# A gated linear recurrence and a squared-ReLU layer on one core: token rows laid out as 16 gaps, 96 head rows, 16 gaps, other transfers for weights and last heads, and a new order of the work up to group 4

## Chip, cores and metric

The kernel runs on one core of one Trainium2 chip. The metric is the device time of that core in microseconds (us): the median of repeated executions. Lower is better.

## What is computed

For 4 sequences, 8 heads, 768 steps and head size 48, a complex gated recurrence is run, and its output, 3072 tokens of 384 features, goes through two products with a squared ReLU between:

```python
S_re, S_im = a_re * S_re - a_im * S_im + k v^T,  a_re * S_im + a_im * S_re   # a limited to |a| < 0.999
y[t] = q[t] @ S_re
x = y as (3072, 384);  out = square(max(x @ w_in, 0)) @ w_out                 # w_in 384 x 2048, w_out 2048 x 384
```

The two weights arrive as 64-bit floats and are turned into 32-bit ones on the chip.

## The kernel before

Tokens are worked in 24 chunks of 128; two chunks are a group, so there are 12 groups (gi). A chunk's 8 heads lie as 4 pairs: in each half of the 128 partitions, rows 0 to 47 hold one head (`rows`), and the 16 rows after them are a gap (`pads`). Three pairs use the head rows. The fourth pair, the "last heads", is loaded into the gaps, a third of each head in each of three slots, so that the elementwise work has no empty rows. TensorE needs the last heads in head rows, so after the elementwise work `last_heads` (L879) copies them there by DMA, from the tile qk to the tile last. In the same way the features of the last heads in the token tile x are copied into its gap rows by `fill_gaps` (L1014), so that the first product has 3 full blocks of 128 rows.

All work is issued in an order written out by hand, the string list FRONT, which `follow` reads token by token; every engine takes its instructions in that order, and waits at the first one that isn't ready. The letters that matter, with group and step behind them:

- p, q: elementwise steps of chunk 0 and chunk 1 of groups 0 and 1 (o: of both chunks at once, from group 2). Steps 0 to 2 and 6 are ACT (squares L750, reordered copies L735); 3 is L764; 7 the inverse (L482, L782); 8 to 10 limit, lessened and grown factor on ACT (L735, L735, L796); 11 gates (L802, L482, L806); 13 grow (L822, L482); 15, 16 and 23 to 27 steps in blocks, 17 totals, 19 carried, 20 and 28 to 30 the four products that write qk (all L482 on DVE, the line of the helper tt); 21 the last heads' DMAs.
- a, b: chunk 0 and chunk 1 of a group on TensorE: 0 scores (L913, L921), 1 and 3 transposes (L928), 2 and 4 their copies on ACT, 5 the mask (DVE, L482), 6 sums of values (L947), 7 tokens into x (ACT, L956), 8 the state's products (L969) with the prod copy on POOL (L975), 9 the new state (DVE).
- g: gap copy. F and H: first product (L1022 by chunk, L1038 by group) and squared ReLU on ACT. T: second product of groups 0 and 1 (L1058). X, Y, Q, Z, R: second product of later groups (L1128), with sums on DVE.
- f, j: load of a block of weight words, block 0 to 7 of w_in and 8 to 15 of w_out; f on SP, j on POOL's queue, half of the rows of w_in each (L669). U, S (ACT, L600, L607), D, A (DVE, L614 and a custom instruction at L482): turning the words of a block into 32-bit floats. Three buffers hold words; a load waits for the buffer's earlier block.
- l, i: load of raw inputs (L507, gaps L517), v: of values (L528), s: store of results (L1092), M: memsets, mask and the first load of the activation table (L546 to L558).

SP's queue takes l, f, v, g, s and the last heads in the order of FRONT. TensorE's F of two chunks and four steps (F0.0.0 to F0.3.0) use blocks 0,1 / 2,3 / 4,5 / 6,7 of w_in.

A step of the elementwise work and the last heads' copies read:

```python
def last_heads():
    for hh in range(HH):
        for g in range(NG):
            at = slice(hh * ROWS + g, hh * ROWS + D, NG)
            nc.sync.dma_start(out=last[gi % 2][at, :, bs, 0:C + 1],
                              in_=qk[pads(hh), :, :, g, 0:C + 1])
```

Of the kernel before, what the change touches and what calls it, by code (L numbers as in the profile page):

```python
# [30 lines left out]
P = 128  # L31
# [395 lines left out]
def quotient_path(ctx, tc, feat, vtok, w_in, w_out, w1, w2, out, n_seq, count):  # L427
# [59 lines left out]
    vt = [const.tile([C, DM + PAD], F32, name=f"vt{i}") for i in range(2 * GC)]  # L487
# [55 lines left out]
    def turn_mask(step):  # L543
# [4 lines left out]
        if step > 1:  # L548

            for t in {2: [begun], 3: [t[:, :, :, :, C:W] for t in qk_of], 4: last,  # L550
                      5: [t[:, DM:] for t in vt] + prod, 6: kt, 7: states[0], 8: states[1]}[step]:
                nc.vector.memset(t, 0.0)
            return
# [14 lines left out]
    qk_of = [const.tile([P, 4, GC, NG, W], F32, name=f"qk{i}") for i in range(2)]  # L568
    last = [const.tile([P, 4, GC, W], F32, name=f"last{i}") for i in range(2)]
    prod = [const.tile([P, 3, GC, NP], F32, name=f"prod{i}") for i in range(2)]  # L570

    states = [[const.tile([P, 2, NP, ROWS], F32, name=f"state{b}{i}") for i in range(2)]
# [69 lines left out]

    def block(i):

        return order[i] == "2", order[:i].count(order[i])

    def fetch(i, second=False):
        of_w2, j = block(i)
        f, fbs = slice(j * BLK, (j + 1) * BLK), slice(j * 2, (j + 1) * 2)
        if (w_out if of_w2 else w_in).dtype == F32:  # L650
            if second:
                return
            if of_w2:
                nc.sync.dma_start(out=w2[:, fbs], in_=w2_view(w_out)[:, fbs])
            else:
                for at, gs, src in w1_views(w_in, D, crossed=True):
                    nc.sync.dma_start(out=w1_blocks[at, j, gs], in_=src[:, :, f])
            return
# [6 lines left out]
        else:  # L665
            for at, gs, src in w1_views(w_in, D, crossed=True):
                if (at.start >= ROWS) != second:
                    continue
                (other if second else nc.sync).dma_start(  # L669
                    out=words[at].rearrange("p (g f) w -> p g (f w)", g=NG)[:, gs],  # L670
# [41 lines left out]
    def make_operands(gi, only=None):  # L712
# [6 lines left out]
        qk, pd = qk_of[gi % 2][:, :, bs], prod[gi % 2][:, :, bs]  # L719
# [11 lines left out]
        by = [qk[:, i, :, :, 0:C].rearrange("p b g (j n) -> p (b g) j n", j=L) for i in range(4)]  # L731
# [116 lines left out]
        def carries():  # L848
# [5 lines left out]
            nc.scalar.copy(out=qk[:, 0:2, :, :, C], in_=at_end)  # L854
# [19 lines left out]
        def last_heads():  # L874
            for hh in range(HH):
                for g in range(NG):

                    at = slice(hh * ROWS + g, hh * ROWS + D, NG)
                    nc.sync.dma_start(out=last[gi % 2][at, :, bs, 0:C + 1],  # L879
                                      in_=qk[pads(hh), :, :, g, 0:C + 1])  # L880
# [11 lines left out]
    def chunk(gi, b):  # L892
# [7 lines left out]
        def scores():  # L900
            qk = qk_of[gi % 2]

            def operand(i, p_, at):
                return last[gi % 2][at, i, b, 0:C] if p_ == NG else qk[at, i, b, p_, 0:C]
# [3 lines left out]
            if not first:  # L908
                for two in range(0, NP, 2):
                    for c in (RE, IM):  # L910
                        for hh in range(HH):
                            for p_ in (two, two + 1):
                                nc.tensor.matmul(  # L913
                                    ys[p_ % 2][crossed(hh, p_), p_ // 2],
                                    lhsT=states[b][1 - c_seq % 2][rows(hh), c, p_],
# [9 lines left out]
        def keys_turned(c):  # L925
            tp = tiles["tp"] = pm.tile([C, NG, P], F32, tag="m", name="tp")
            for g in range(NG):
                nc.tensor.transpose(tp[:, g], qk_of[gi % 2][:, 2 + c, b, g, 0:C], ident)  # L928
# [14 lines left out]
        def sums_of_values():  # L943
            for p_ in range(NP):
                for hh in range(HH):
                    at = (HH * p_ + hh) * D
                    nc.tensor.matmul(tiles["y"][p_ % 2][crossed(hh, p_), p_ // 2],  # L947
                                     lhsT=v[:, at:at + ROWS], rhs=tiles["am"][:, hh, p_],
# [3 lines left out]
        def tokens():  # L952
            if gi not in x_of:
                x_of[gi] = ffn.tile([P, NP, TOK], F32, name="x")
            for odd in range(2):
                nc.scalar.copy(out=x_of[gi][:, odd::2, b * C:(b + 1) * C],  # L956
                               in_=tiles["y"][odd][:, 0:NP // 2])

        def added():
# [5 lines left out]
            for c in (RE, IM):  # L965
                for p_ in range(NP):
                    for hh in range(HH):
                        rr, at = slice(hh * ROWS, (hh + 1) * ROWS), (HH * p_ + hh) * D
# [3 lines left out]
        def last_products():  # L972
            bs = slice(b, b + 1) if gi < BY_CHUNK else slice(0, GC)
            pd, end = prod[gi % 2][:, :, bs], last[gi % 2][:, 0:2, bs, C]
# [4 lines left out]
        def new_state():  # L979
            before, new = [states[b][i][:, :, :, 0:D] for i in (1 - c_seq % 2, c_seq % 2)]  # L980
# [30 lines left out]
    def fill_gaps(i, b=None):  # L1011
        x = x_of[i] if b is None else x_of[i][:, :, b * C:(b + 1) * C]
        for hh in range(HH):
            nc.sync.dma_start(out=x[pads(hh), 0:NG], in_=x[rows(hh), NG])  # L1014
# [117 lines left out]
    def outputs(i, r):  # L1132
# [30 lines left out]
        "M7 M8 l0.0.0 M4 M2 M3 l0.0.1 M0 M1 p0.0 p0.2 p0.3 p0.4 p0.5 p0.7 q0.0 M6 q0.3 p0.9 "  # L1163
        "p0.8 p0.1 q0.4 p0.10 q0.5 p0.11 l0.1.0 f0 q0.7 i0.1.1 j0 i0.1.0 j1 j2 p0.12 p0.22 q0.8 "
        "q0.10 U0 q0.1 q0.9 q0.2 S0 f1 U1 S1 p0.15 p0.23 D0 p0.24 p0.13 p0.25 q0.11 p0.16 A0 "
        "p0.26 D1 f2 l0.1.1 f3 p0.27 M5 A1 p0.17 q0.22 p0.6 q0.13 p0.14 q0.12 q0.15 U2 p0.18 "
        "q0.14 S2 p0.19 q0.23 D2 l1.2.0 f4 i1.2.0 j4 j3 j5 q0.24 p0.28 q0.25 p0.20 q0.16 p0.29 "
        "q0.26 p0.30 q0.27 q0.17 a0.3 p0.21 a0.4 q0.6 i1.2.1 a0.1 p1.6 U3 q0.18 A2 U4 a0.2 S3 "
        "q0.19 D3 q0.28 q0.20 p1.0 S4 p1.3 p1.4 p1.5 a0.0 q0.29 q0.30 a0.5 v0.0 l1.2.1 f5 p1.1 "
        "p1.2 q0.21 a0.8 a0.6 p1.7 q1.0 a0.9 D4 A3 b0.3 b0.0 p1.8 a0.7 p1.10 p1.9 q1.1 U5 p1.11 "  # L1170
        "q1.3 A4 b0.5 p1.12 b0.4 S5 p1.15 p1.22 b0.1 b0.2 q1.4 p1.13 p1.23 D5 q1.5 j7 j6 g0.0 "
        "f6 f7 v0.1 q1.6 U6 p1.14 F0.1.0 S6 p1.24 A5 p1.25 D6 p1.16 U7 H0.1.0 S7 D7 p1.26 A6 "
        "p1.27 f9 f8 F0.2.0 b0.8 b0.6 A7 b0.7 H0.2.0 U9 U8 p1.17 p1.18 q1.7 F0.0.0 F0.3.0 "
        "H0.0.0 p1.19 D8 p1.20 p1.28 D9 p1.29 g0.1 f10 D10 p1.30 F0.3.1 q1.10 S8 H0.3.0 H0.3.1 "
        "S9 v1 f12 f11 q1.9 q1.2 A8 b0.9 F0.1.1 F0.2.1 A9 a1.1 T0.0.0 q1.8 U10 q1.11 a1.2 S10 "
        "U11 q1.12 D11 D12 q1.15 A10 q1.23 p1.21 a1.3 T0.1.0 a1.0 S11 q1.22 H0.1.1 f13 f15 "
        "F0.0.1 q1.13 q1.24 a1.5 q1.25 D13 q1.16 A11 a1.6 U12 a1.4 q1.14 S12 a1.7 a1.8 q1.26 "
        "A12 q1.27 q1.17 T0.2.0 T0.3.0 T0.4.0 U13 H0.2.1 H0.0.1 S13 q1.18 A13 g1.0 F1.3.0 i2 "
        "q1.19 q1.20 q1.28 q1.29 q1.30 f14 U15 U14 S14 H1.3.0 l2 q1.21 o2.0 S15 D14 D15 A14 "
        "o2.3 A15 o2.1 o2.4 o2.5 a1.9 o2.7 T0.5.0 F1.1.0 F1.2.0 T0.6.0 T0.7.0 b1.1 o2.2 E0.0 "  # L1180
        "b1.2 o2.8 o2.9 b1.0 b1.5 b1.3 H1.1.0 T0.0.1 T0.1.1 F1.0.0 o2.10 o2.11 o2.12 o2.15 b1.4 "
        "o2.23 o2.22 o2.13 o2.24 o2.25 o2.16 o2.26 b1.6 b1.8 T0.2.1 T0.3.1 T0.4.1 b1.7 o2.27 "
        "o2.17 T0.5.1 T0.6.1 T0.7.1 o2.14 H1.0.0 o2.6 E0.1 w0 g1.1 o2.18 o2.19 o2.28 o2.20 "
        "o2.29 o2.30 s0.0 l3 o2.21 v2 F1.1.1 H1.1.1 H1.2.0 T1.0.0 T1.1.0 F1.2.1 T1.2.0 T1.3.0 "
        "T1.4.0 T1.5.0 b1.9 a2.3 F1.0.1 o3.6 H1.2.1 a2.4 a2.1 T1.6.0 o3.0 o3.1 o3.3 a2.0 a2.5 "
        "a2.2 o3.4 o3.5 H1.0.1 o3.7 t0 T1.7.0 a2.6 a2.8 a2.7 b2.0 b2.5 a2.9 W0 o3.9 o3.8 o3.2 "
        "E1.0 F1.3.1 b2.3 b2.4 b2.6 T1.0.1 T1.1.1 T1.2.1 T1.3.1 H1.3.1 b2.7 g2 F2.1 F2.6 T1.4.1 "
        "T1.5.1 o3.10 o3.11 o3.12 o3.15 o3.23 o3.24 o3.25 o3.22 o3.13 o3.16 o3.26 o3.27 o3.14 "
# [182 lines left out]
```

## Time and profile before

| | |
|---|---|
| median of 3 runs | 670.68 us (669.2 to 671.22) |
| profiled execution | 671.83 us, its span 670.0 us |
| busy: TensorE matmul, weight load | 617.4 us (92%), 552.3 us (82%) |
| busy: VectorE (DVE), ScalarE (ACT), GpSimd (POOL) | 496.4 us (74%), 421.7 us (63%), 35.3 us (5%) |
| mean granted TensorE clock | 0.992 |
| DMA | 60.37 MB, 49231 packets |
| last heads' DMAs | 24 of 32.2 KB, 60 of 64.5 KB, all on SP |
| w_in words' DMAs | 24 on SP and 24 on POOL, six to a block of 768 KB |

The engine rows of the page cut the span into 40 slices of 16.75 us; each digit is the busy share of a slice in tenths. A timeline line gives the start, the length, engine and line, the operation, what it writes and reads, and in brackets how long the engine had been idle before it and what ended that. In the chain of waits each line is a start, a length and the piece of work that held up the end. Lines with a q (SPq, ACTq) are queues: the time in which an engine issues a DMA.

### The profile page before, as it was taken

To read this page: it belongs to the slowest core of one execution; us is meant where nothing else is said; L and a number is where in the kernel's file an instruction comes from. 1 tells how busy PE (TensorE), PEld (TensorE's weight loads), DVE (VectorE), ACT (ScalarE), POOL (GpSimd) and SP (SyncE) were. 2 spreads that over 40 slices of the span, in tenths; PEclk is the share of its full clock that TensorE was granted. 3 is DMA by queue.
4 is the path that set the end of the run, shared out by engine and by line. 5 is a ranking of instruction groups with operands and counts; after the bars stand their busy time and mean duration, and the time that the engine had idled before them with its cause. 6 is when DMAs were issued, how large, how long until landed. Compare 5 with 4: busy or idle time off the path is not lost.

```text
span 670.0 us, 13180 instructions
## 1 busy us (share of the span) xinstructions
PE 617.4 (92%) x5147; PEld 552.3 (82%) x5147; DVE 496.4 (74%) x973; ACT 421.7 (63%) x822; POOL 35.3 (5%) x82
## 2 busy tenths in 40 slices
PE   0058999999999999999999999999999999999996
PEld 0047987777789989989989999899989899989995
DVE  7998996967979868959849958978948957753030
ACT  7669988566475477484486686586585584544331
POOL 6331030000000000000000000000000000000000
PEclk9997999999999999999999999999999999999998
DMA  8897783360630740830742631632741720233101
GB/s 194 161 155 154 228 212 65 57 94 18 110 65 8 131 103 5 125 72 8 129 130 73 117 78 46 127 83 80 129 95 31 108 50 35 66 74 88 47 25 29
DMA packets 49231, 60.37 MB, mean 90 GB/s; under 512 B 6792, under 2 KB 40072, under 8 KB 49160
## 3 DMA queue, kind: packets, MB, share of 16 engines
q1 hardware_dynamic: 46336, 53.78, 38.4%
q0 software_dynamic: 2336, 5.21, 4.1%
q8 instruction: 42, 0.69, 0.4%
q10 hardware_dynamic: 488, 0.44, 0.2%
q14 instruction: 29, 0.24, 0.1%
HBM read 48.76 MB, written 4.72 MB: 80 GB/s over the span
## 4 chain that ended last, share of the span: by engine, by line
PE 86%; DMA 6%; DVE 2%; SPq 2%; issue 1%; ACT 1%; POOL 0%; ACTq 0%; POOLq 0%
PE h_ps L1038 31%; PE o_ps L1128 28%; PE a_ps L921 6%; PE h_ps L1022 5%; PE o_ps L1058 5%; PE y L947 3%; PE y L913 3%; PE add L969 3%; DMA raw<-in_feat_dram 2%; DMA words<-in_moe_w_in_dram 2%; PE tp L928 2%; DMA last<-qk 1%; SPq L879 1%; DMA words<-in_moe_w_out_dram 1%; SPq L669 1%
## 5 line engine op out<-in xcount | busy, mean ns | idle before, releaser
L1038 PE MATMUL h_ps<-x,w 128*128 128x256 f32 x960 | 212.3, 380 | 0.1
L1038 PEld LDWEIGHTS h_ps<-x,w 128*128 128x128 f32 x960 | 181.1, 190 | 25.0 <-issue 0.4
L1128 PE MATMUL o_ps<-w,h 128*128 128x192 f32 x640 | 110.4, 328 | 0.0
L1128 PEld LDWEIGHTS o_ps<-w,h 128*128 128x128 f32 x640 | 103.8, 190 | 1.9 <-issue 0.9
L1045 ACT ACTIVATE h<-h_ps 128x512 f32<-128x512 f32 x80 | 47.5, 594 | 68.8 <-PE h_ps L1038 67.5
L482 DVE TENSOR_TENSOR pr<-ab 128x384 f32<-128x384 f32 (+3 forms) x196 | 70.0, 375 | 4.1 <-ACT ab L810 0.9
L482 DVE TENSOR_TENSOR a<-a_ps,mask 128x1024 f32<-128x1024 f32 x24 | 29.3, 1223 | 40.2 <-PE a_ps L921 40.1
L1128 PE MATMUL o_ps<-w_sum,mix 128*128 128x192 f32 x320 | 55.5, 328 | 0.0
L482 DVE TENSOR_TENSOR ab<-pr 128x48 f32<-128x48 f32 (+3 forms) x210 | 49.9, 259 | 5.3
L1128 PEld LDWEIGHTS o_ps<-w_sum,mix 128*128 128x128 f32 x320 | 51.7, 190 | 0.9 <-issue 0.3
L1046 ACT ACTIVATE h<-h 128x512 f32<-128x512 f32 x80 | 50.4, 631 | 2.6
L928 PE MATMUL tp<-ident,qk 128*128 128x128 f32 x120 | 21.8, 294 | 32.0 <-DVE qk L482 31.3
L1022 PEld LDWEIGHTS h_ps<-x,w 128*128 128x128 f32 x384 | 45.7, 198 | 1.7 <-ACT h L1028 0.2
L482 DVE TENSOR_TENSOR qk<-ab,qk 128x768 f32<-128x768 f32 (+1 forms) x56 | 46.1, 842 | 1.0
L1022 PE MATMUL h_ps<-x,w 128*128 128x128 f32 x384 | 46.4, 281 | 0.0
L1058 PE MATMUL o_ps<-w,h 128*128 128x384 f32 x128 | 44.3, 490 | 1.6 <-DVE w L482 1.6
L928 PEld LDWEIGHTS tp<-ident,qk 128*128 128x128 f32 x120 | 15.2, 148 | 36.6 <-issue 32.5
L735 ACT ACTIVATE qk<-raw 128x768 f32<-128x768 f32 (+1 forms) x28 | 37.1, 1344 | 11.8 <-DVE raw L482 6.4
L921 PE MATMUL a_ps<-qk 48*128 48x128 f32 x576 | 40.0, 287 | 0.0
L482 DVE TENSOR_TENSOR room<-ab,carry 128x1344 f32<-128x1344 f32 (+1 forms) x28 | 36.8, 1354 | 3.8 <-ACT carry L851 3.4
L482 DVE TENSOR_TENSOR mix<-h 128x256 f32<-128x256 f32 x40 | 16.8, 420 | 30.7 <-ACT h L1046 30.7
L921 PEld LDWEIGHTS a_ps<-qk 48*128 48x128 f32 x576 | 35.3, 194 | 4.5 <-issue 4.4
(105 smaller groups left out, 911.2 us busy)
## 6 DMA issues: line engine op xcount, KB each, us to landing
raw<-in_feat_dram SPq DMA_DIRECT2D x40, 288.0 KB
words<-in_moe_w_out_dram SPq DMA_DIRECT2D x8, 768.0 KB
again<-in_moe_w_in_dram SPq DMA_DIRECT2D x16, 384.0 KB
again<-in_moe_w_out_dram SPq DMA_DIRECT2D x16, 384.0 KB
vt<-in_vtok_dram SPq DMA_DIRECT2D x24, 192.0 KB
out_dram<-o SPq DMA_DIRECT2D x23, 192.0 KB
last<-qk SPq DMA_DIRECT2D x60, 64.5 KB
raw<-in_feat_dram SPq DMA_DIRECT2D x120, 32.0 KB
```

Of the source, the lines that this page charges most:

```text
L482: nc.vector.tensor_tensor(out=out, in0=in0, in1=in1, op=op)
L735: nc.scalar.activation(out=out.rearrange("p c j n -> p c n j"), func=AF.Copy, in_=in_.rearrange("p c (n j) -> p c n j", j=L), **kwargs)
L913: nc.tensor.matmul(ys[p_ % 2][crossed(hh, p_), p_ // 2], lhsT=states[b][1 - c_seq % 2][rows(hh), c, p_], rhs=operand(c, p_, rows(hh)), sta ...
L921: nc.tensor.matmul(ps[:, hh, p_], lhsT=operand(2 + c, p_, rows(hh)), rhs=operand(c, p_, rows(hh)), start=(c == RE), stop=(c == IM))
L928: nc.tensor.transpose(tp[:, g], qk_of[gi % 2][:, 2 + c, b, g, 0:C], ident)
L947: nc.tensor.matmul(tiles["y"][p_ % 2][crossed(hh, p_), p_ // 2], lhsT=v[:, at:at + ROWS], rhs=tiles["am"][:, hh, p_], start=(first and p_ ...
L1022: nc.tensor.matmul(ps[:, j], lhsT=w1_blocks[:, k, g, at:at + P], rhs=x_of[i][:, g, b * C:(b + 1) * C], start=(g == 0), stop=(g == NG - 1))
L1038: nc.tensor.matmul(ps[:, j], lhsT=w1_blocks[:, k, g, at:at + P], rhs=x_of[i][:, g], start=(g == 0), stop=(g == NG - 1))
L1045: nc.scalar.activation(out=h, in_=h_ps[i, f], func=AF.Relu, scale=of_w1)
L1046: nc.scalar.activation(out=h, in_=h, func=AF.Square)
L1058: nc.tensor.matmul(o_of[i, b], lhsT=tokens_of(i, f, b)[:, j], rhs=w2[:, k], start=(k == 0), stop=(k == NFB - 1))
L1128: nc.tensor.matmul(to, lhsT=x(k)[:, j], rhs=factor(z)[:, 2 * k + j], start=(z in (0, 1, 3) and k == j == 0), stop=(k == KH // 2 - 1 and j ...
```

## The change

Rows: the values' tile vt gets 16 zero columns ahead of the features as well as behind. With the helper `columns`, the upper half of the partitions takes its 64 columns from 16 columns earlier, so that the upper half of y has the gap first and the head rows after it. A token tile is then 16 gap rows, 96 head rows, 16 gap rows (`token_rows`, `token_pads`). The state tiles are laid out flat for the same reason. Copying tokens to x for the odd pairs now swaps the halves, as two copies of 64 partitions, where one copy of 128 did before: three ACT copies to a chunk in place of two.

Words of w_in: a block comes as one transfer of 96 rows on SP and two of 16 rows on POOL, in place of three on each queue.

Last heads: qk and last are laid out with the four parts of a row beside each other; a chunk's last heads are 2 transfers of 48 rows of 2080 bytes, where it was 6 transfers (each 16 rows by 4 parts of 516 bytes; from group 2 on, for both chunks at once).

Memsets: of the states, last and kt only the columns that nothing else writes are cleared; vt has two strips to a tile.

Order: FRONT is new up to the first product of group 4, the same after it. The core of the diff:

```diff
@@ -469,9 +469,21 @@
+    def columns(hh, at):
+        at -= PAD * (1 - hh)
+        return slice(at, at + ROWS)
+    def token_rows(hh):
+        return slice(PAD, ROWS) if hh == 0 else slice(ROWS, ROWS + D)
+    def token_pads(hh):
+        return slice(0, PAD) if hh == 0 else slice(ROWS + D, P)
...
@@ -484,7 +496,7 @@
-    vt = [const.tile([C, DM + PAD], F32, name=f"vt{i}") for i in range(2 * GC)]
+    vt = [const.tile([C, PAD + DM + PAD], F32, name=f"vt{i}") for i in range(2 * GC)]
...
@@ -547,8 +559,11 @@
-            for t in {2: [begun], 3: [t[:, :, :, :, C:W] for t in qk_of], 4: last,
-                      5: [t[:, DM:] for t in vt] + prod, 6: kt, 7: states[0], 8: states[1]}[step]:
+            for t in {2: [begun], 3: [t[:, :, :, :, C:W] for t in qk_of],
+                      4: [t[:, :, 0:2, C] for t in last], 5: [t[:, at:at + PAD] for t in vt for at in (0, PAD + DM)] + prod,
+                      6: [t[:, NG].rearrange("p (hh x) -> p hh x", hh=HH)[:, :, D:ROWS] for t in kt],
+                      7: [x for t in states[0] for x in (by_pair(t)[..., 0:PAD], t[:, :, NP * ROWS:])],
+                      8: [x for t in states[1] for x in (by_pair(t)[..., 0:PAD], t[:, :, NP * ROWS:])]}[step]:
...
@@ -565,11 +580,14 @@
-    qk_of = [const.tile([P, 4, GC, NG, W], F32, name=f"qk{i}") for i in range(2)]
-    last = [const.tile([P, 4, GC, W], F32, name=f"last{i}") for i in range(2)]
+    qk_of = [const.tile([P, GC, NG, 4, W], F32, name=f"qk{i}") for i in range(2)]
+    last = [const.tile([P, GC, 4, W], F32, name=f"last{i}") for i in range(2)]
-    states = [[const.tile([P, 2, NP, ROWS], F32, name=f"state{b}{i}") for i in range(2)]
+    def by_pair(t):
+        return t[:, :, 0:NP * ROWS].rearrange("p c (n e) -> p c n e", n=NP)
+    states = [[const.tile([P, 2, NP * ROWS + PAD], F32, name=f"state{b}{i}") for i in range(2)]
...
@@ -639,6 +657,13 @@
+    def w1_rows():
+        cut = NG * HH * D
+        rest = w_in[cut:].rearrange("(hh r g) f -> hh r g f", hh=HH, g=NG)
+        return [(slice(PAD, ROWS + D), w_in[0:cut].rearrange("(g r) f -> r g f", g=NG))] + [
+            (token_pads(hh), rest[hh]) for hh in range(HH)]
...
@@ -663,11 +688,9 @@
-            for at, gs, src in w1_views(w_in, D, crossed=True):
-                if (at.start >= ROWS) != second:
-                    continue
+            for at, src in w1_rows()[second:3 if second else 1]:
-                    out=words[at].rearrange("p (g f) w -> p g (f w)", g=NG)[:, gs],
+                    out=words[at].rearrange("p (g f) w -> p g (f w)", g=NG),
...
@@ -728,7 +751,7 @@
-        by = [qk[:, i, :, :, 0:C].rearrange("p b g (j n) -> p (b g) j n", j=L) for i in range(4)]
+        by = [qk[:, :, :, i, 0:C].rearrange("p b g (j n) -> p (b g) j n", j=L) for i in range(4)]
...
@@ -851,7 +874,7 @@
-            nc.scalar.copy(out=qk[:, 0:2, :, :, C], in_=at_end)
+            nc.scalar.copy(out=qk[:, :, :, 0:2, C].rearrange("p b g c -> p c b g"), in_=at_end)
...
@@ -872,12 +895,12 @@
-            for hh in range(HH):
-                for g in range(NG):
-                    at = slice(hh * ROWS + g, hh * ROWS + D, NG)
-                    nc.sync.dma_start(out=last[gi % 2][at, :, bs, 0:C + 1],
-                                      in_=qk[pads(hh), :, :, g, 0:C + 1])
+            for b in range(bs.start, bs.stop):
+                for hh in range(HH):
+                    nc.sync.dma_start(
+                        out=last[gi % 2][rows(hh), b].rearrange("p x t -> p (x t)"),
+                        in_=qk_of[gi % 2][pads(hh), b].rearrange("p g x t -> p g (x t)"))
...
@@ -901,7 +924,7 @@
-                return last[gi % 2][at, i, b, 0:C] if p_ == NG else qk[at, i, b, p_, 0:C]
+                return last[gi % 2][at, b, i, 0:C] if p_ == NG else qk[at, b, p_, i, 0:C]
...
@@ -912,7 +935,7 @@
-                                    lhsT=states[b][1 - c_seq % 2][rows(hh), c, p_],
+                                    lhsT=states[b][1 - c_seq % 2][rows(hh), c, columns(hh, p_ * ROWS + PAD)],
...
@@ -953,8 +976,10 @@
-                nc.scalar.copy(out=x_of[gi][:, odd::2, b * C:(b + 1) * C],
-                               in_=tiles["y"][odd][:, 0:NP // 2])
+                for to, of in [(slice(0, P), slice(0, P))] if not odd else [
+                        (slice(0, ROWS), slice(ROWS, P)), (slice(ROWS, P), slice(0, ROWS))]:
+                    nc.scalar.copy(out=x_of[gi][to, odd::2, b * C:(b + 1) * C],
+                                   in_=tiles["y"][odd][of, 0:NP // 2])
...
@@ -965,19 +990,19 @@
-            pd, end = prod[gi % 2][:, :, bs], last[gi % 2][:, 0:2, bs, C]
+            pd, end = prod[gi % 2][:, :, bs], last[gi % 2][:, bs, 0:2, C].rearrange("p b x -> p x b")
...
@@ -1011,7 +1036,7 @@
-            nc.sync.dma_start(out=x[pads(hh), 0:NG], in_=x[rows(hh), NG])
+            nc.sync.dma_start(out=x[token_pads(hh), 0:NG], in_=x[token_rows(hh), NG])
...
@@ -1160,54 +1185,54 @@
-        "M7 M8 l0.0.0 M4 M2 M3 l0.0.1 M0 M1 p0.0 p0.2 p0.3 p0.4 p0.5 p0.7 q0.0 M6 q0.3 p0.9 "
-        "p0.8 p0.1 q0.4 p0.10 q0.5 p0.11 l0.1.0 f0 q0.7 i0.1.1 j0 i0.1.0 j1 j2 p0.12 p0.22 q0.8 "
-        "q0.10 U0 q0.1 q0.9 q0.2 S0 f1 U1 S1 p0.15 p0.23 D0 p0.24 p0.13 p0.25 q0.11 p0.16 A0 "
-        "p0.26 D1 f2 l0.1.1 f3 p0.27 M5 A1 p0.17 q0.22 p0.6 q0.13 p0.14 q0.12 q0.15 U2 p0.18 "
-        "q0.14 S2 p0.19 q0.23 D2 l1.2.0 f4 i1.2.0 j4 j3 j5 q0.24 p0.28 q0.25 p0.20 q0.16 p0.29 "
-        "q0.26 p0.30 q0.27 q0.17 a0.3 p0.21 a0.4 q0.6 i1.2.1 a0.1 p1.6 U3 q0.18 A2 U4 a0.2 S3 "
-        "q0.19 D3 q0.28 q0.20 p1.0 S4 p1.3 p1.4 p1.5 a0.0 q0.29 q0.30 a0.5 v0.0 l1.2.1 f5 p1.1 "
-        "p1.2 q0.21 a0.8 a0.6 p1.7 q1.0 a0.9 D4 A3 b0.3 b0.0 p1.8 a0.7 p1.10 p1.9 q1.1 U5 p1.11 "
-        "q1.3 A4 b0.5 p1.12 b0.4 S5 p1.15 p1.22 b0.1 b0.2 q1.4 p1.13 p1.23 D5 q1.5 j7 j6 g0.0 "
-        "f6 f7 v0.1 q1.6 U6 p1.14 F0.1.0 S6 p1.24 A5 p1.25 D6 p1.16 U7 H0.1.0 S7 D7 p1.26 A6 "
-        "p1.27 f9 f8 F0.2.0 b0.8 b0.6 A7 b0.7 H0.2.0 U9 U8 p1.17 p1.18 q1.7 F0.0.0 F0.3.0 "
-        "H0.0.0 p1.19 D8 p1.20 p1.28 D9 p1.29 g0.1 f10 D10 p1.30 F0.3.1 q1.10 S8 H0.3.0 H0.3.1 "
-        "S9 v1 f12 f11 q1.9 q1.2 A8 b0.9 F0.1.1 F0.2.1 A9 a1.1 T0.0.0 q1.8 U10 q1.11 a1.2 S10 "
...
+        "M8 l0.0.0 M2 M3 M7 l0.0.1 M1 M0 p0.0 p0.1 p0.3 p0.4 p0.5 p0.7 p0.2 q0.0 q0.3 p0.8 p0.9 "
+        "p0.10 q0.4 q0.5 p0.11 q0.7 l0.1.0 f0 f1 l0.1.1 v0.0 f2 i0.1.0 j0 j2 q0.1 p0.12 p0.22 "
+        "q0.8 q0.2 U0 q0.9 p0.6 q0.10 S0 p0.15 p0.23 p0.24 D0 p0.25 M4 p0.13 M5 p0.16 q0.11 "
+        "p0.26 i0.1.1 j1 D1 p0.27 A0 p0.17 p0.14 j3 i1.2.0 U1 S1 U2 q0.12 p0.18 q0.6 S2 q0.22 "
+        "A1 f4 l1.2.0 f3 j4 p0.19 q0.15 p0.20 q0.23 p0.28 q0.24 p0.29 q0.25 p0.30 q0.16 D2 "
+        "q0.26 q0.13 q0.27 A2 q0.17 p0.21 f6 a0.1 a0.2 U3 q0.14 a0.0 a0.3 U4 S3 q0.18 p1.6 a0.4 "
+        "S4 a0.5 a0.6 l1.2.1 a0.7 D3 q0.19 M6 a0.8 q0.28 q0.20 p1.0 p1.3 q0.29 D4 q0.30 i1.2.1 "
+        "q1.0 p1.4 p1.5 j6 j5 p1.1 p1.2 j7 g0.0 f5 v0.1 q0.21 f7 p1.7 p1.10 p1.9 p1.8 A3 A4 "
+        "F0.1.0 U5 a0.9 U6 S5 D5 b0.1 b0.0 p1.11 b0.2 p1.12 S6 H0.1.0 A5 U7 b0.3 b0.4 S7 p1.15 "
+        "D6 p1.23 b0.5 F0.0.0 b0.6 b0.7 f8 p1.24 A6 p1.25 q1.3 p1.16 D7 p1.26 A7 p1.27 D8 p1.17 "
+        "F0.2.0 H0.0.0 q1.4 H0.2.0 U8 p1.22 S8 F0.3.0 b0.8 H0.3.0 p1.18 p1.13 p1.14 A8 g0.1 f11 "
+        "F0.2.1 f9 f10 v1 p1.19 p1.20 p1.28 D9 p1.29 p1.30 q1.5 U9 q1.1 H0.2.1 q1.7 D11 b0.9 "
+        "D10 F0.3.1 T0.0.0 H0.3.1 S9 A9 U10 q1.8 S10 q1.9 q1.2 q1.10 F0.0.1 F0.1.1 p1.21 f12 "
...
```

## The prediction

> **What bounds the kernel now.** I read the page's busy rows first, then the table by stages, cut where the chain of waits turns from transfers to TensorE.
>
> ```profile
> PE   0058999999999999999999999999999999999996
> ...
> DVE  7998996967979868959849958978948957753030
> ...
> PEclk9997999999999999999999999999999999999998
> DMA  8897783360630740830742631632741720233101
> ```
>
> ```profile
> 0.00:57.11 57.11, 13.22 (x117) 10.80 (x117) 50.50 (x131) 40.42 (x80) 24.17 (x52) 0.99 0.86 167
> 57.11:160.00 102.89, 100.50 (x945) 83.76 (x946) 84.72 (x168) 78.37 (x137) 7.45 (x16) 0.98 0.55 124
> 160.00:660.00 500.00, 499.90 (x4066) 454.32 (x4065) 360.84 (x674) 302.62 (x606) 3.69 (x14) 1.00 0.37 75
> 660.00:670.00 10.00, 3.76 (x24) 3.47 (x22) 0.36 (x1) 0.33 (x1) 0.00 (x0) 0.82 0.19 49
> ```
>
> The columns are stage, length, then busy PE, PEld, DVE, ACT, POOL. TensorE's idle time is 57.11 - 13.22 = 43.9 us ahead of 57.11, 2.4 us to 160, 0.1 us to 660, 6.2 us at the end. The instruction order is the same from group 4's first product on, and both programs issue 2634 matmuls from the FRONT list. So only 43.9 + 2.4 us can move: this is a change to the first 110 us, and the other edits on full stages are worth nothing. In the first stage DVE is busy 50.5 of 57.1 us and the transfer engines 86%: both are near a limit. The chain of waits and the timelines by engine show the order:
>
> ```profile
> 51.80 5.17 DMA last<-qk
> 57.11 1.19 PE a_ps L921 x6
> ```
>
> ```profile
> 10.30 1.03 DVE L552 MEMSET kt<- 128x512 f32 x2
> ...
> 11.83 0.56 DVE L802 SCALAR_TENSOR_TENSOR room<-room 128x384 f32<-128x384 f32 x1
> ...
> 47.43 1.23 DVE L482 TENSOR_TENSOR a<-a_ps,mask 128x1024 f32<-128x1024 f32 x1 [0.24 <-PE a_ps L921]
> ...
> 68.33 0.95 DVE L482 CUSTOM_DVE_ANT_0 w<-w,part 128x1536 uint16<-128x1536 uint16 x1
> ...
> 107.82 0.96 DVE L764 SCALAR_TENSOR_TENSOR room<-room 128x768 f32<-128x768 f32 x1 [3.13 <-ACT room L750]
> ```
>
> ```profile
> 37.80 3.87 SPq L879 DMA_DIRECT2D last<-qk  x6
> ...
> 47.26 6.04 SPq L879 DMA_DIRECT2D last<-qk  x6
> 53.39 1.23 SPq L1014 DMA_DIRECT2D x<-x  x2
> ```
>
> ```profile
> 49.06 1.94 PE L947 MATMUL y<-a,vt 128*64 128x128 f32 x16
> ...
> 58.92 7.11 PE L1022 MATMUL h_ps<-x,w 128*128 128x128 f32 x48
> ...
> 109.79 1.56 PE L1058 MATMUL o_ps<-w,h 128*128 128x384 f32 x4 [1.64 <-DVE w L482]
> ```
>
> Between 11.83 and 47.43 DVE waits once, 0.24 us: the first masking (a0.5) is paced by DVE's queue, with the last heads (landed at 46.2) barely ahead of it. The six issues of chunk 1's last heads hold SP to 53.3, so the gap copy of chunk 0's tokens, ready at 52.2, starts at 53.39; and TensorE's first F stands in its order behind chunk 1's scores, which wait for 5.17 us of transfer.
>
> **The change, part by part.**
>
> **Second table load.** The new order runs M1 before M0, and the built program has two table loads where it had one. The row is
>
> ```profile
> 3.27 1.28 ACT L546 ACT_TABLE_LOAD   x1 [3.27 <-issue]
> ...
> 6.42 0.84 ACT L750 ACTIVATE room<-raw 128x768 f32<-128x768 f32 x1 [0.43 <-DMA raw<-in_feat_dram]
> ```
>
> One more 1.28 us ahead of the squares, of which the 0.43 us wait for raw absorbs its part: squares at 7.3, not 6.42 (+0.9). Against this the Trainium skill ("ScalarE: Activation LUTs", What ACT_TABLE_LOAD costs) also has 1283 ns for the instruction, but its rules for kernel authors budget about 2.7 us a switch. By that, squares come at 8.7 and every number below is 1.4 us later (gain 2.6 in place of 4.0). In this trace the next ACTIVATE starts 1.29 us after the load began, so I take the row.
>
> **Fewer memsets.** Only kt (1.03 us at 10.30) lay inside DVE's busy queue; the states (2.11) and last (2 x 0.93) ran while DVE waited for ACT, worth nothing. kt's place now is a wait: gates needs ACT's L735 pair (limit, lessened), which the table load pushes to 12.8. Gates start at 12.8, not 11.83: the saved microsecond is spent there. Eight more memsets, each under 0.1 us, replace them.
>
> **DVE's order to the first mask.** From gates to a0.5 is 35.4 us without waits. Moved behind a0.5: carried of chunk 1 (1.62 + 0.86, 2.43 start to start), its four products (0.47 each), a D (0.48) and L764 of the next group (0.5): 5.3. Nothing is moved ahead except about 0.2 of small memsets. DVE is ready at 12.8 + 35.4 - 5.3 + 0.2 = 43.1.
>
> **Last heads.** Chunk 0's products now end 7.0 us of DVE work (two steps and D 1.6, grow 1.46, a step 0.6, an A 0.87, totals 2.5) before a0.5: at 36.1 (37.7 before). Two issues of 0.6 in place of six: the last at 36.7. Before, six 16 x 4 x 129 transfers (384 rows of 516 B) landed 4.5 us after the issues ended; now 96 rows of 2080 B. Bounds for landing: 2.04 us (the pair 104.28 to 106.31 in the chain, little traffic) and 5.17 (at 51.80, full traffic). So 38.7 to 41.9. Here the skill speaks against a gain: "DMA: Bandwidth & Descriptors", Specifications, puts line rate at rows of 512 B or more, which 516 B already reach; and its fit (2.0 us + bytes/436e9) would land the old set at about 43.2 as an estimate (41.07 + 2.0 + 0.1). It landed at 46.2: under this traffic the rule is short by 3 us, so I use the rows. Scores' part that needs no last heads ends near 40 (36.2 + tp 0.9 + 2.93); the rest costs 1.8 at the low clock. Mask at 43.1 to 43.7, say 43.3; before 47.43.
>
> **To the first F.** Mask ends 44.5, y (1.94) 46.5. Tokens are three ACT copies in place of two, two of them of 64 partitions and the same length: 0.3 us more (0.65 for a pair of 0.37), x at 47.5. Over the run that is 24 x 0.3 = 7 us of ACT, hidden where ACT waits 67.5 us for TensorE at L1045. SP is free, so the gap copy issues 47.5 to 48.7 and lands 2.0 to 5.2 after its second issue: 50 to 53.3, take 51.3. The first F is now ahead of chunk 1's scores. TensorE resumes at 51.3 against 57.11, but has 1.9 us less behind it (one tp 0.33 and 26 of 32 score matmuls, 1.6, at full clock): gain 3.9 here.
>
> **w1's words.** Six transfers a block become three, 16 fewer SP issues (about 0.5 each) and 8 fewer on POOL; bytes and 2 KB rows stay, so transfer time stays. 576 of 768 KB now sit on SP, behind its waits: block 5's and chunk 1's values and last heads queue behind the gap copy, which waits for x. Block 5 issues at 48.8 and lands 4 to 7.3 us later (7.27 at 10.03): 53 to 56, DVE wants it at 54.9. On POOL the prod copy, waiting for last heads, now stands ahead of half of chunk 1's next raw load: issued about 42.5 to 44.6, landing 4.7 later (median), 49.3; ACT wants it at 48.
>
> **DVE to the last w1 block (A7).** From 44.5: carried 2.43, products 1.9, D3 to D7 2.4, A3 to A7 4.35, new state 1.55, the second mask 1.14, L764 twice 1.0, inverse 1.08, gates 1.95, six steps 3.5, kt's memset 0.1: 21.4. With 1.3 of waits for block 5 and ACT, A7 starts at 66.3 and ends at 67.2 (before 68.33 to 69.19). F0.3.0 waits for it: four F and both adds are done at 67.2 + 2.66 + 0.95 = 70.8; before, at 67.92 + 2 x 2.72 = 73.4. So the 3.9 shrinks to 2.6 by here.
>
> **The gaps after.** Before, A15 stood behind L764, which waited 3.13 us for ACT; TensorE waited 1.64. Now D15 and A15 stand ahead of it, and one F (2.66 us) more stands ahead of T0.7.0: that wait goes. At 149 TensorE waited 0.53 for the next last heads (six issues, 5.13 us on SP, now four): gone. Against both, 0.7 for new short waits (POOL's raw load, block 5's fetch). The low clock of slice 4 (PEclk 7) is paid once either way.
>
> **Sum.** 2.6 + 1.6 + 0.5 - 0.7 = 4.0 us. The profiled execution took 671.83 (span 670.0 and 1.8 around it): 667.8. The median of runs is 1.15 lower, 670.68: **666.7**.
>
> **Rivals.**
> - *DVE's total paces the front* (0.10): block 5 or POOL's load comes late by its bound, A7 is at 69, the lead 0.8, and waits for decode take the place of the old gaps. For it: DVE is busy 19 us of 20 through 100 us. Against: A15 no longer waits behind ACT. About 0.8 gained: 669.9.
> - *Slower* (0.05): SP's single queue. The gap copy's wait holds block 5's 96 rows; if they land after about 59.5, A5, A6, A7 slip by more than the 4.0 gained, and F0.2.0 and F0.3.0 with them. At a landing of 62 that is +2.5: 673.2. It would take 11 us from issue; the longest words transfer in the trace took 9.0.
> - *More than summed* (0.07): transfers lose 2 x 384 short rows and land at 2 us; first F at 49.8 and A7 at 65: 5.4 + 2.4 and about 1.5 from earlier decode: 661.4.
> - That the order doesn't do what it says is excluded by the built program's order.
>
> **How the numbers follow.** The likeliest case (0.78) spans 663 (5.4 + 2.4) to 669.2 (lead 1.5, no gaps closed). The range 661.8 to 669.6 adds part of the neighbours. A difference under 0.3% (2.0 us) can't be told from none: faster is 0.77 of the likeliest case and the 0.07, 0.84; same is its last 0.01 and DVE's 0.10, 0.11; slower 0.05.
>
> **What would show it.** Two table loads and squares near 7.3; first mask near 43.3; last heads landing within 5.2 us of their second issue; first F near 51.3; A7's end near 67.2 with F0.3.0 starting on it; no 1.6 us wait at T0.7.0; idle 2.4 or less from 57 to 160; stages after 160 unchanged. It is wrong if DVE waits over 2 us between 44 and 67, or if the tail differs.

## The result, and the profile after

The changed kernel takes 665.36 us (median of 4 runs, 664.94 to 666.06); the kernel before, beside it, 670.81 (4 runs). The ratio is 0.9924, with a 95% interval of 0.9906 to 0.9943: 5.4 us faster, where 4.0 was forecast. The profiled execution took 666.06 us, with a span of 664.1.

The same rows of the page, after:

```profile
PE   0068999999999999999999999999999999999996
...
DVE  4999888979997969858849948968849858753030
...
PEclk9998999999999999999999999999999999999999
DMA  8986863540634331730842813542631620232101
```

The table by stages of the changed kernel (stage, length, then busy PE, PEld, DVE, ACT, POOL; at the end granted clock, transfer engines' share and GB/s), the last cut moved with the end:

```profile
0.00:57.11 57.11, 15.71 (x144) 13.34 (x145) 47.32 (x141) 42.72 (x83) 20.39 (x46) 1.00 0.90 180
57.11:160.00 102.89, 102.89 (x947) 83.94 (x943) 90.03 (x174) 84.14 (x149) 7.24 (x15) 0.98 0.49 116
160.00:654.00 494.00, 494.00 (x4038) 450.89 (x4037) 355.51 (x667) 307.70 (x617) 4.25 (x14) 1.00 0.36 76
654.00:664.10 10.10, 4.10 (x26) 3.81 (x24) 0.36 (x1) 0.33 (x1) 0.00 (x0) 0.88 0.18 49
```

TensorE is idle 57.11 - 15.71 = 41.4 us ahead of 57.11 (43.9 before), then not at all until 654 (2.4 + 0.1 before), and 6.0 at the end (6.2). That is 5.2 us less idle time; TensorE's busy time fell by 0.7 (617.4 to 616.7). Part of it may be a shorter stretch of matmuls at half rate (the granted clock is 0.50 from about 55.5 to 62 us before, and from about 57.5 to 61 now), but no run separates it. 5.2 + 0.7 is the 5.9 by which the span fell.

The front, from the changed kernel's timelines. TensorE, from chunk 0's y on (start, length, tile, count, and in brackets the idle time ahead with what ended it):

```profile
43.57 1.97 PE L970 MATMUL y<-a,vt 128*64 128x128 f32 x16 [2.57 <-DVE a L494]
...
48.77 1.58 PE L1047 MATMUL h_ps<-x,w 128*128 128x128 f32 x12 [1.12 <-DMA x<-x]
51.42 1.60 PE L1047 MATMUL h_ps<-x,w 128*128 128x128 f32 x12 [1.08 <-DVE w L494]
...
56.79 0.71 PE L944 MATMUL a_ps<-last 48*128 48x128 f32 x6 [0.27 <-DMA last<-qk]
...
58.05 4.24 PE L1047 MATMUL h_ps<-x,w 128*128 128x128 f32 x24
...
68.80 1.14 PE L994 MATMUL add<-vt,kt 128*64 128x48 f32 x32
69.86 5.62 PE L1047 MATMUL h_ps<-x,w 128*128 128x128 f32 x48
```

DVE's first mask and its last w1 block (A7), SP's queue between, and ACT's second table load with the squares behind it:

```profile
42.30 1.22 DVE L494 TENSOR_TENSOR a<-a_ps,mask 128x1024 f32<-128x1024 f32 x1
...
63.73 0.95 DVE L494 CUSTOM_DVE_ANT_0 w<-w,part 128x1536 uint16<-128x1536 uint16 x1
```

```profile
35.46 1.32 SPq L901 DMA_DIRECT2D last<-qk  x2
...
39.38 0.32 SPq L519 DMA_DIRECT2D raw<-in_feat_dram  x1
...
46.00 1.28 SPq L1039 DMA_DIRECT2D x<-x  x2
```

```profile
5.93 1.28 ACT L558 ACT_TABLE_LOAD   x1
...
7.33 0.83 ACT L773 ACTIVATE room<-raw 128x768 f32<-128x768 f32 x1
```

The first F starts 10.2 us earlier than before (48.77 against 58.92), but only one F moved that far: chunk 1's scores now stand behind it, and the four F and both adds are done at 69.86, against 73.4 before. That lead of 3.5 us, the two gaps of 1.64 and 0.53 us that closed, and 0.2 at the end are the 5.9. Two lines of before for this: 73.4 is where the first 48 of the 120 matmuls of the first line end, and the 0.53 is in the brackets of the second.

```profile
67.92 13.66 PE L1022 MATMUL h_ps<-x,w 128*128 128x128 f32 x120
...
149.38 0.29 PE L913 MATMUL y<-last,state 48*64 48x128 f32 x1 [0.53 <-issue]
```

### The profile page after: what moved, and what is told of

It reads as the page before. It is cut to its first block, busy times and chain, and to the rows that moved or that the text cites. A ratio compares the mean times of both kernels' runs of the same rounds, so it can differ in the third digit from the quotient of the medians.

```text
span 664.1 us, 13108 instructions
## 1 busy us (share of the span) xinstructions
PE 616.7 (93%) x5147; PEld 552.0 (83%) x5147; DVE 493.2 (74%) x981; ACT 434.9 (65%) x847; POOL 31.9 (5%) x74
## 4 chain that ended last, share of the span: by engine, by line
PE 91%; DVE 5%; DMA 2%; ACT 1%; issue 1%; ACTq 0%; POOL 0%; DVEq 0%; SPq 0%
PE h_ps L1063 31%; PE o_ps L1153 28%; PE a_ps L944 7%; PE o_ps L1083 6%; PE h_ps L1047 6%; PE y L970 4%; PE y L936 3%; PE add L994 3%; PE tp L951 2%; DVE ab L494 1%; DMA last<-qk 1%; DVE pr L494 1%; DMA raw<-in_feat_dram 1%; DVE qk L494 0%; DMA words<-in_moe_w_in_dram 0%
## 5 line engine op out<-in xcount | busy, mean ns | idle before, releaser
L494 DVE TENSOR_TENSOR ab<-pr 128x48 f32<-128x48 f32 (+3 forms) x210 | 49.9, 260 | 5.3
L981 ACT COPY x<-y 64x256 f32<-64x256 f32 (+1 forms) x72 | 26.5, 368 | 24.9 <-PE y L970 23.4
```

The source lines that it names most:

```text
L494: nc.vector.tensor_tensor(out=out, in0=in0, in1=in1, op=op)
L981: nc.scalar.copy(out=x_of[gi][to, odd::2, b * C:(b + 1) * C], in_=tiles["y"][odd][of, 0:NP // 2])
```

## Experiments

Each was timed in several executions beside the kernel before, but for experiment 6, which ran once and is read by its timeline alone. "Changed" is the changed kernel at 665.36 and 0.9924. It was timed in another set than the variants, and the kernel before took 669.98 to 670.88 us in the sets, so a difference of under 1 us between two variants says little.

**1. New parts, old order.** The FRONT list of before, all else changed.

> The new layout, transfers, copies and memsets, but the instruction order of before. Theory (the order carries most of the gain): the first mask is still paced by DVE at about 47.2 to 47.4 us, the last heads' shorter issue frees SP about 2.6 us earlier, so chunk 1's last heads land at 53 to 55.5 instead of 57.1 and the first F comes at 56.5 to 57.5 instead of 58.92; one table load. Gain over the kernel before 1.0 to 2.4 us: a ratio of 0.9965 to 0.9985, that is 668.4 to 669.7 us. Rival (the transfers carry the gain): at least 3.5 of the 5.4 us stay, 667 us or less.

667.50 us, ratio 0.996 (0.9946 to 0.9974). Chunk 1's last heads hold nothing up any more, and the first F comes at 55.65 (58.92 before). So parts without order give 2.5 us by the medians, a little over the theory's range; the order is worth another 2.1. That is net of the second table load, which the new order brings and this variant does not have (experiment 10).

**2. New order, old parts.** The kernel before with the FRONT list of after. (Its full memset of kt now stands behind the copy of chunk 0's keys and clears them.)

> The kernel before, with its transfers, copies and full memsets, but the new instruction order. Theory: six issues of 0.65 us from 35.4 us on and 4.5 us of landing bring chunk 0's last heads at about 43.5 to 44, so that the first mask waits for them to about 45 (42.30 in the changed kernel, 47.43 before); chunk 1's last heads land about 2.5 us later than in the changed kernel. Gain over the kernel before 2 to 3.5 us, a ratio of 0.995 to 0.997, 667.2 to 668.7 us. Rival (order alone does it, the transfers are beside the path): within 1 us of the changed kernel, a ratio of 0.992 to 0.9935.

674.91 us, ratio 1.0076 (1.0057 to 1.0096): slower than before, against both expectations. The timeline of TensorE:

```profile
43.08 1.19 PE L921 MATMUL a_ps<-last 48*128 48x128 f32 x6 [1.13 <-DMA last<-qk]
...
54.95 5.46 PE L1022 MATMUL h_ps<-x,w 128*128 128x128 f32 x24 [3.60 <-DMA x<-x]
```

The last heads come as the theory said (43.1). But the mask, at 44.58 for 42.30, did not wait for them. In this order the old, full memsets of the two tiles of `last` lie in DVE's busy queue, which only the new parts shorten:

```profile
19.07 0.93 DVE L552 MEMSET last<- 128x1040 f32 x1 [0.17 <-DMA raw<-in_feat_dram]
```

The second one follows at 20.16. What the theory missed besides is the gap copy: SP issued it at 48.28 to 49.52, 2.3 us later than in the changed kernel, and it landed at 54.9. The full memset of kt, at 48.77, holds TensorE for another 1.57 us. Alone the new order loses; it needs the other parts, and this run does not separate the transfers from the memsets.

**3 and 4. Six transfers for each chunk's last heads**, with rows of 516 bytes (as before), and with rows of 2080.

The edit for short rows; for long ones both sides are whole, `last[at, b]` and `qk[pads(hh), b, g]`:

```
             for b in range(bs.start, bs.stop):
                 for hh in range(HH):
...
-                    nc.sync.dma_start(
-                        out=last[gi % 2][rows(hh), b].rearrange("p x t -> p (x t)"),
-                        in_=qk_of[gi % 2][pads(hh), b].rearrange("p g x t -> p g (x t)"))
+                    for g in range(NG):
+                        at = slice(hh * ROWS + g, hh * ROWS + D, NG)
+                        nc.sync.dma_start(out=last[gi % 2][at, b, :, 0:C + 1],
+                                          in_=qk_of[gi % 2][pads(hh), b, g, :, 0:C + 1])
```

> The changed kernel, with each chunk's last heads moved by six transfers of 16 x 4 rows of 516 bytes, as before. If the short rows cost what they cost before (4.5 us from the last issue to landing), chunk 0's land at about 43.5 to 44 and the mask goes from 42.30 to about 45; chunk 1's land near 59 instead of 56.8. 2.5 to 3.5 us slower than the changed kernel: a ratio to the kernel before of 0.996 to 0.9975. Rival (only the number of issues counts): the same time as the variant with six transfers of long rows, with landing within 3 us of the last issue.

> The changed kernel, with each chunk's last heads moved by six transfers of 16 rows of 2080 bytes: as many rows and bytes as the two transfers, three times the issues. The theory that both issues and rows count: issues end 2.6 us later than with two, landing stays near 3 us, so chunk 0's last heads land near 41.7, the mask waits 0.5 to 1 us, chunk 1's land 2.6 us later: 1 to 2.5 us slower than the changed kernel, a ratio to the kernel before of 0.994 to 0.9965, and faster than the variant with short rows by about 1 us. Rival (rows alone count): the time of the changed kernel, ratio 0.992 to 0.993.

677.56 us (1.0113, 1.009 to 1.0136) and 675.40 (1.0084, 1.0061 to 1.0106): 12 and 10 us slower than changed, far beyond all that was expected. The row length, whose intervals overlap, is the small part. But chunk 0's scores waited only to 40.93 and 40.81, and the mask stayed at 42.30: the transfer that was meant to be slow did not hold up the mask. Part of the loss was the variant's own: from group 2 on it issued 12 transfers a group (before had 6), and 4 to 5 us of idle time came up between 160 and 640.

**5. Six long-row transfers in the first two groups only.** The loop of 4 under `if gi < BY_CHUNK`, and the changed kernel's two transfers a chunk otherwise.

> As the variant with six transfers of long rows, but only in the first two groups (the front); from group 2 on each group has the changed kernel's four transfers. In the variant with six everywhere the gap copy of chunk 0's tokens, issued at 46.0 us as in the changed kernel, landed 3.4 us later, and later groups, with 12 issues each, waited too. Theory (the front's share is what the changed kernel saves): first F at 52.2, the four F and adds done at 70.8 (69.86 in the changed kernel), waits of about 1.4 us in 75 to 110, no idle time from 160 to 640: 2 to 3 us slower than the changed kernel, 667.4 to 668.4 us, a ratio to the kernel before of 0.995 to 0.997. Rival (the front is as costly as it looked in sum): 5 us or more slower than the changed kernel, a ratio over 0.999.

670.49 us, ratio 1.0001 (0.999 to 1.0011): 5.1 us slower than changed, the rival's size. So this one edit is worth as much as the whole change. TensorE in this variant:

```profile
40.78 1.19 PE L952 MATMUL a_ps<-last 48*128 48x128 f32 x6 [1.09 <-DMA last<-qk]
...
52.77 5.46 PE L1055 MATMUL h_ps<-x,w 128*128 128x128 f32 x24 [4.91 <-DMA x<-x]
```

Mask and x are where they were (chunk 0's scores, 1.7 us later, still end ahead of the mask); the gap copy was issued at 45.99 as in the changed kernel (46.00), and landed 4 us later. The table of a window in this variant, and then in the changed kernel:

```profile
36.00:40.00 4.00, 3.69 (x28) 3.07 (x27) 3.90 (x9) 2.59 (x6) 0.00 (x0) 1.00 0.21 46
```

```profile
36.00:40.00 4.00, 4.00 (x34) 3.54 (x33) 3.90 (x9) 2.58 (x6) 0.95 (x2) 1.00 0.74 157
```

While SP spends 3.8 us on six small transfers, it issues no large one: the transfer engines are 0.21 busy and move 46 GB/s in place of 157. That is (157 - 46) x 4 us = 444 KB less, 2.4 us of work at the 185 GB/s that follow from 40 to 46 us (an estimate); POOL's half of the next load also starts 1.4 us later (41.49 for 40.09), behind its copy of the last heads. Both loads then lie ahead of the gap copy. DVE waits 3.12 us for ACT, which waits for that load.

The late gap copy is only part of the 5.1 us: the four F and both adds are done at 71.28, 1.4 us behind the changed kernel. About 2 us more come in group 1, which has six transfers too: SP spends 5.05 us on them (1.32 in the changed kernel) and issues the next words 5.3 us later (83.99 for 78.72), and TensorE waits 2.0 us between 75 and 115, for words and for the last heads themselves, where the changed kernel waits for nothing:

```profile
78.83 5.05 SPq L903 DMA_DIRECT2D last<-qk  x6
```

```profile
85.42 0.29 PE L944 MATMUL y<-last,state 48*64 48x128 f32 x1 [1.06 <-DMA last<-qk]
```

**6. The gap copy ahead of the load**, in variant 5. The second chunk of the next group is squared from old data here, since its load comes after.

```
-a0.6 l1.2.1 a0.7
...
-g0.0 f5
+a0.6 a0.7
...
+g0.0 l1.2.1 f5
```

> The variant with six long-row transfers in the first two groups, with SP's half of the load of the next group's second chunk (288 KB and 96 KB) moved behind chunk 0's gap copy. Theory (a transfer lands when the bytes put into SP's queue ahead of it are through; six slow issues leave the transfer engines idle and push the load and the gap copy back): the gap copy, issued at 46.0 as before, lands before 49, and the first F starts at 48 to 49 instead of 52.2. The whole run is slower, since the load itself comes 6 us later. Rival (the small transfers are slow by themselves, by their rows and the traffic of all queues): the first F stays at 51.5 or later.

```profile
49.98 4.66 PE L1055 MATMUL h_ps<-x,w 128*128 128x128 f32 x24 [2.11 <-DMA x<-x]
```

With SP's 384 KB behind it the copy lands 2.8 us earlier, at 49.9. That is between the two expectations, nearer the theory's 49: bytes ahead delay it, and POOL's half of the load is still ahead.

**7. More work for DVE** between the first mask and A7: one block's first decode step five times (D5 becomes D5 D5 D5 D5 D5).

> The changed kernel, with the first decode step of one block of w1 done five times instead of once, at 53.7 us on DVE (the same result): 4 x 0.47 = 1.9 us more for DVE between the first mask and the last w1 block. Theory (DVE has cover there now: the second mask, the blocks A5 and A7 all end ahead of their use): A5 ends near 63.0 and A7 near 66.5, TensorE waits at most 0.6 us for A7, and nothing after 70: 0 to 0.6 us slower than the changed kernel, a ratio to the kernel before of 0.992 to 0.9935. Rival (DVE's sum paces the front, as the prediction had it for F0.3.0): 1.9 us slower, a ratio of 0.995 to 0.9955.

668.04 us, ratio 0.9959 (0.9944 to 0.9974): 2.7 us slower than changed, for 1.9 us of work. The theory falls: DVE has no cover there. TensorE's timeline, where the changed kernel waits for nothing:

```profile
62.76 1.98 PE L970 MATMUL y<-a,vt 128*64 128x128 f32 x16 [2.38 <-DVE a L494]
```

The second mask went from 58.54 to 61.49, and TensorE waited for it. In this trace the gap copy also landed 0.6 us later than in the changed kernel (first F at 49.43), with the same order up to there, so a part of the 2.7 may not be DVE's.

**8. A second F ahead of chunk 1's scores.** F0.0.0 directly in front of F0.1.0; H0.0.0 and H0.1.0 exchanged.

> The changed kernel with F0.0.0 put directly ahead of F0.1.0, before chunk 1's scores, and the two squared relus exchanged. F0.0.0 needs only blocks 0 and 1, long decoded. Theory: the waits of 1.08 us (block 3), 0.29 us and 0.93 us (chunk 1's last heads) in TensorE's queue between 51 and 57 go, 2.3 us; about 0.9 of it comes back as a wait of F0.3.0 for A7, which ends at 64.6: 1.0 to 2.0 us faster than the changed kernel, 663.4 to 664.4 us, a ratio to the kernel before of 0.989 to 0.991. Rival (DVE and ACT follow the second chunk's scores, so what TensorE gains is waited for at the second mask and after): the changed kernel's time or slower, a ratio of 0.992 to 0.994.

665.78 us, ratio 0.9928 (0.9908 to 0.9948): the rival, no gain.

```profile
49.40 8.35 PE L1047 MATMUL h_ps<-x,w 128*128 128x128 f32 x48 [1.59 <-DMA x<-x]
...
62.02 1.09 PE L970 MATMUL y<-a,vt 128*64 128x128 f32 x16 [1.48 <-DVE a L494]
```

The 2.3 us of waits are gone, but 48 matmuls took 8.35 us (5.62 for 48 elsewhere), and the second mask, whose scores now stand behind two F, is waited for.

**9. Six transfers for each block's words**, three on SP and three on POOL.

> The changed kernel, with each block's w1 words moved by six transfers as before: three on SP (384 KB) and three on POOL (384 KB) in place of one of 576 KB on SP and two of 96 KB on POOL. Theory (an issue costs only where it leaves the transfer engines without bytes): three issues of about 0.5 us for 384 KB still put more bytes into the queue than leave it, so the number of issues is worth nothing, and the bytes that go from SP's queue to POOL's move landings by under 1 us: within 1 us of the changed kernel, a ratio to the kernel before of 0.991 to 0.994. Rival (issues cost here what they cost with the last heads): 2 to 4 us slower than the changed kernel, 0.9955 to 0.998.

667.64 us, ratio 0.9958 (0.9944 to 0.9972): 2.3 us slower than changed, the rival's lower end. Its trace again has the gap copy late, with issue at 46.29:

```profile
52.59 4.81 PE L1052 MATMUL h_ps<-x,w 128*128 128x128 f32 x24 [4.48 <-DMA x<-x]
```

Between 40 and 42 us the engines are 0.37 busy (81 GB/s): SP's part of the block, 384 KB for 576, is through before the next load is issued at 40.29; the rest of the block's bytes has gone to POOL, where it comes later, ahead of the gap copy. In this trace the four F and both adds are done only 0.6 us later than in the changed kernel, so the front accounts for 0.6 of the 2.3 us; where the rest arises is not settled.

**10. One table load** (M0 ahead of M1).

> The changed kernel with M0 ahead of M1: one table load instead of two. Theory (a load costs its 1.28 us row, of which 0.9 reaches the squares, and DVE's sum paces the front): squares at 6.4, DVE's wait of 0.82 us for the gates goes, first mask 0.7 to 0.9 earlier, at 41.5; 0.4 to 1.0 us faster than the changed kernel, a ratio to the kernel before of 0.991 to 0.992. By the Trainium skill's budget of 2.7 us per switch (ScalarE: Activation LUTs, What ACT_TABLE_LOAD costs) 2 us or more would be gained: 0.989 or less. Rival (transfers pace the front, so that DVE waits for words what it gained): the changed kernel's time, 0.9920 to 0.993.

664.11 us, ratio 0.9902 (0.9886 to 0.9917): 1.25 us below the changed kernel's median, and their intervals overlap; a little more than the theory's 1.0, and less than the 2 of the budget. Squares begin at 5.85 (7.33), gates at 11.30 (12.76), the mask at 40.84 (42.30). DVE's wait ahead of the gates did not go, as the theory had it (0.83 us); the first F, at 48.53, now waits 2.16 us for the gap copy.

**11 and 12. Four moves in the order** (one table load; kt's memset into DVE's first idle time; chunk 1's four products together; A3 ahead of the next group's inverse), and the same with chunk 0's gap copy issued by ACT.

```
-M7 l0.0.1 M1 M0
+M7 M6 l0.0.1 M0 M1
...
-q0.19 M6 a0.8 q0.28 q0.20 p1.0 p1.3 q0.29 D4 q0.30 i1.2.1
+q0.19 a0.8 q0.28 q0.20 q0.29 q0.30 p1.0 p1.3 D4 i1.2.1
...
-p1.7 p1.10 p1.9 p1.8 A3 A4
+A3 p1.7 p1.10 p1.9 p1.8 A4
```

In the second of the two, g0.0 stands directly behind a0.7, and its transfers are issued on ACT's queue.

> The changed kernel with four moves in the order: M0 ahead of M1 (one table load), the kt memset in DVE's idle time at the start, chunk 1's four products directly behind its carry step (ahead of a decode and the next group's first step), and block 3's second decode step ahead of the next group's inverse. Theory: first mask at 41.5, chunk 1's last heads ready 1 to 1.8 us earlier, no wait for kt (0.35) and little for block 3 (1.08); the first F as early as the gap copy allows. 1.5 to 3 us faster than the changed kernel, a ratio to the kernel before of 0.988 to 0.990. Rival (SP's queue holds the gap copy at 48.8 or later, and DVE's sum to A7 is the same but for the table load): 0.5 to 1 us faster, 0.991 to 0.992.

> The variant with the four moves, and chunk 0's gap copy issued by ACT directly behind its x copies, so that it is in another queue than the load of the next group. Theory (on SP it stands behind the bytes of that load): it lands within 2.5 us of its second issue, the first F starts 0.5 to 1.5 us earlier than with SP; ACT spends 1.2 us on the issues, ahead of the next group's squares. 0 to 1 us faster than the variant with the four moves. Rival (the transfer engines are full, so the queue makes no difference): the first F not earlier, and ACT's 1.2 us makes it slower by up to 1 us.

663.93 us, ratio 0.9899 (0.9884 to 0.9914), and 668.39, ratio 0.9965 (0.995 to 0.998). The four moves reach the theory's ratio, but experiment 10 comes within 0.0003 of them with the table load alone: the other three moves gave nothing that can be told. The waits for kt and block 3 went, but the first F waits 2.18 us for the gap copy (the rival's mechanism, though its 48.8 is not met: 47.94), and its matmuls then ran slow. Experiments 10 and 11 are the fastest kernels of the study. On ACT's queue the copy is the worst of all:

```profile
45.17 1.28 ACTq L1039 DMA_DIRECT2D x<-x  x2
```

```profile
54.38 4.85 PE L1047 MATMUL h_ps<-x,w 128*128 128x128 f32 x24 [7.99 <-DMA x<-x]
```

With the copy gone from SP, SP no longer waits there for x, and issues block 5 (576 KB) and the values (192 KB) at 43.22 and 43.58, ahead of it. So another queue was no way out here. The 768 KB more that were issued ahead would take 4.2 us at the 185 GB/s of experiment 5 (an estimate), and the copy landed 5.6 us later than in the changed kernel: the bytes that the engines were given before, on any queue, are most of it. In which order they serve several queues is not settled by these runs.

## Why the prediction was right, and where it was not

- **Bound and order of size: right.** Only the front moved; nothing after group 4 changed, and the lead and the later gaps carry the result.
- **Table load: mis-sized.** Squares came at 7.33 as predicted (7.3). But one load less puts them at 5.85, so the load costs 1.48 in this order, not 0.9. The Trainium skill's 2.7 us a switch ("ScalarE: Activation LUTs", What ACT_TABLE_LOAD costs) was too high here: the time fell by 1.25 us with one load less.
- **Mask: 43.3 predicted, 42.30 measured.** Gates at 12.76 as predicted (12.8); the sum from there was 0.8 too long. The last heads were not waited for, as predicted: chunk 0's landed within 2.3 us of SP's last issue.
- **Later landing: outside the bounds.** Chunk 1's last heads took 6.7 us, beyond the 5.17 that the prediction gave as the upper bound. The chain of waits of the changed kernel has the piece:

```profile
50.05 6.70 DMA last<-qk
```

The fit that the prediction set aside ("DMA: Bandwidth & Descriptors" of the Trainium skill, Anatomy of one DMA) is given there for transfers that GpSimd issues. The last heads are issued on SP, so the 3 us by which it missed do not test it.

- **First F: 51.3 predicted.** Its first half started at 48.77, because the gap copy took about 2 us from its second issue, the lower bound; its second half waited 1.08 us for block 3, which the prediction did not have, to 51.42. The two misses cancel for the most part (the first F ends at 53.0; 51.3 + 2.66 = 54.0 by the prediction), and that is luck.
- **A7: 67.2 predicted, 64.68 measured.** 1.0 is the earlier mask, 1.3 are the waits for block 5 and ACT, which did not come; the rest is other small terms. So F0.3.0 did not start on A7, and the lead is 3.5 in place of 2.6. The wait that DVE does set is the second mask's, which ends 2.5 us ahead of its use; in experiment 7, with 1.9 us more DVE work, that mask came 2.95 us later and the margin was gone.
- **Later gaps: both gone (1.64 and 0.53), as predicted; new waits: 0.7 predicted, none measured.** So 3.5 + 2.2, and 0.2 at the end, in place of 2.6 + 2.1 - 0.7: 5.9 by the spans, of which the medians show 5.4.
- **The parts were not weighed as they count, though the sum held.** For the words the prediction said that "bytes and 2 KB rows stay, so transfer time stays". For the last heads it counted their landing and SP's issue time ("SP is free"), and left out the large transfers that SP could not issue in that time. Both edits are worth more (2.3 and 5.1 us with the rest of the change in place). For the last heads the runs show why in good part (experiments 5 and 6); for the words only 0.6 us. The order list could have told it: the words f6 (576 KB) and SP's and POOL's loads of the next group (768 KB) stand ahead of the gap copy.
- **The parts do not add up.** Order, words and last heads undone singly cost 2.1, 2.3 and 5.1, together 9.5 of a gain of 5.4. The old words and the old six transfers each make the gap copy late by themselves (52.59 and 52.77 for the first F); the old order does not, since there the first F stands behind chunk 1's scores (55.65). The row layout and the smaller memsets were not undone singly.

## What to carry to other kernels

In this kernel's front, where the transfer engines are near full (0.90 busy), a small transfer landed later the more bytes were issued before it. So cost such a transfer by what is ahead of it, and cost each issue by the large transfers that its queue could have issued in that time. Before a new order is credited with a gain, look at which transfer it puts in front of the first wait of the bound engine. And undo the parts one at a time from the final kernel: here the order alone was a loss (674.91 us), and undoing it in the final kernel costs 2.1.

## What the runs showed of the hardware

TensorE ran slow after some waits, and the granted clock of the page does not always show it. In variant 5 the first F's matmuls, and in the changed kernel those of the stretch from 63 us, by tile (duration min, median, max in ns):

```profile
L1055 PE MATMUL h_ps<-x,w x24: 418/421/553, 52.8 to 57.8; 128*128 128x128 f32 x24
```

```profile
L1047 PE MATMUL h_ps<-x,w x48: 275/275/377, 63.2 to 68.6; 128*128 128x128 f32 x48
```

421 ns in place of 275, and 5.46 us for 24 in place of 2.84 (the F behind it in variant 5): half rate, with a granted clock of 1.00 in the table by windows (52 to 58 us). It is 2.6 us for one F, on top of the wait. The Trainium skill ("TensorE: Matmul & The Clock Gate", Part 1: The HAM clock gate) has the half rate of an idle array and about 3.4 us to warm up; here the slow stretch lasted some 5 us.

How long the last wait was does not decide it alone. In experiments 5, 8 and 10 the F after a wait of 4.91, 1.59 and 2.16 us ran at 421 ns. The changed kernel's first F, after 1.12 us, ran at 275, but its next one, at 58.05, took 4.24 us with no wait directly ahead, with a granted clock of about 0.50 from 57.5 to 61. So the first two F cost 7.4 us of matmuls there and 8.3 in experiments 5, 8 and 10: a stretch at half rate came in each, and what sets its place and length stays open.
